# Attention and gated feed-forward on one core: final copy on two engines, a whole-tile store, GpSimd kept off two blocks, other buffers for two query parts, and new orders

## The chip, the core and the metric

The kernel runs on one core of a Trainium2 chip. The core has five engines that run side by side, each with its own queue of instructions taken strictly in order: TensorE (PE in the profile; PEld is its loading of weights), VectorE (DVE), ScalarE (ACT), GpSimd (POOL) and SyncE (SP). An instruction that waits for a semaphore holds up everything behind it on its engine. Matmuls write to PSUM, and the other engines read it from there; all else lies in SBUF. Transfers to and from memory run on 16 DMA engines and are issued by SP, ACT and POOL. The metric is the time of one execution in microseconds (us), taken over several runs.

## What is computed

The reference has an attention part with a squared ReLU instead of a softmax, and a gated feed-forward part on its output:

```python
# q, k, v: 8 batches x 12 heads x 448 positions x 64, float32
scores = (1 / sqrt(64)) * q @ k.T
attn   = maximum(scores, 0) ** 2 / 448
a      = attn @ v                        # 8 x 12 x 448 x 64
x      = a as 3584 tokens x 768
g      = x @ w_gate                      # 768 x 1536
u      = gelu(g) * (x @ w_val)           # 3584 x 1536
out    = u @ w_out                       # 3584 x 768, float32
```

## The kernel before

**Tiling.** All matmuls work in bfloat16 on quarters of the array: a 64x64 block of weights in one row half and one column half, with 448 moving columns (384 for the output product). `mm` (line 409) issues one. A step issues a pair of them, one for each column half, in the same row half; the plan calls pairs of the upper row half `PE0` and of the lower one `PE1`, and TensorE is fully used while a pair of each runs at the same time. Both are in one queue.

**Stages.** For each batch, heads come in pairs and parts of four heads. `load_qk` (line 461) brings a part of queries and keys to a `qk16` tile (a ring of two buffers in `hpool`), `add_transposes` turns it (on TensorE for the batches 0 and 1 and one part of batch 2, line 676, else by a DMA from a regrouped copy `qkr` in `lpool`, line 518). `add_scores` makes 21 units of scores a batch; ScalarE's ReLU (line 743) and VectorE's square (line 752) turn each into `attnT`. `add_values` multiplies by `v` (one accumulator for each pair of heads) and a copy (lines 814, 825) leaves `xT`. `add_gate_value` makes the dense gate and value products of a block of 128 columns of the hidden layer; other blocks go, for two batches at a time, through `add_pair`, a seven-product scheme (Strassen's) with sums of weights (line 890) and of tokens (line 909). GELU is on ScalarE (lines 985, 1061); the multiply of gate by value (lines 990, 1066) leaves `uT`. In `add_pair` that multiply may also go to GpSimd for the last pair of batches (`b >= SPARED`, line 1006). `add_product` makes the output in 14 groups of two 128-token tiles, again with seven products each, named "1" to "7"; their sums are on VectorE (line 1177), the results are copied or added into `osb` (lines 1265, 1267) and stored (line 1286).

**What sets the order.** The whole program is laid out by `run_plan` when it is built: it places every step by assumed costs and landing times (`margin` is added to a load's assumed landing). Batch 0's front is placed by hand with times (`at` below 0 is before the first dense product); everything after it comes in the order of the string `LINE` (a priority list: "s" scores, "o" values, digits dense products, letters the seven-product units). The loads of weights ("w", "o" for the output weights), "q" and "v" parts come in the order of `LOADS`, all issued by GpSimd, in order. While TensorE would idle in the first 30 us, `fill` (line 583) puts in matmuls on a zero tile `held` (line 597).

**The end.** Unit "3" of the last group is the last to run. Its result is copied by ScalarE alone, and the last group's first tile is stored in column halves, the second tile in two stores of 64 rows, one issued by SP and one by ACT:

```python
        if final and name == "3":
            rd.other = None
        (DVE if added else ACT).append(rd)
        ...
            if final and t == t0:
                SP.append(Op("SP", 0.6, lambda: emit_store(0, nc.sync, cols), reads, prio=-1))
                ACT.append(Op("ACT", 0.5, lambda: emit_store(1, nc.scalar, cols), reads, prio=-1))
```

Of the kernel before, what the change touches and what calls it, by code (L numbers as in the profile page):

```python
# [12 lines left out]
a3 1 s 1 s s o s 2D4 0 s 1 o 0 2A1 s 0F5 o o 0 s f1 2 0F6 s s 0E3 2A3 2 0F4 0 o o o 0 0 0F3 o o o  # L13
0F7 s s 2 a4 1 c6 s s 0 s 0F1 s b1 o 5 d1 d4 6C6 2D6 s s s s 0E2 0F2 0 s c1 s s s s 0 0E5 a7 1 1 s
6F5 2C4 0E1 1 2B1 s 0E7 s 2 0 o 0 0 0E6 1 o 0 1 s 1 f7 s s 0 0E4 4B6 s a1 5 o c4 2 s s s 2F2 b2 s 0
a5 a2 s s s o 0 3 b3 2B4 1 1 s s s 4C4 4 0 s 1 2B5 3 s 1 s o s 1 s 2E7 s 0 c3 s k7 s b4 1 a6 2B2 1
1 6D4 o 1 2A5 2 c7 2D1 o 6A1 2D5 2F1 2 2C3 b7 b5 1 s d6 s s s 3 s 2F3 2B3 b6 2C1 s 4D1 c2 2 s s s
2A4 s 2E4 4A3 s e1 3 s 2E6 2C2 6D7 c5 2B6 2A2 4F6 f5 2 s 2F6 2D2 s 2B7 s 2A6 s s 2D3 o s 4D7 2 s
2C6 2D7 2C5 s 2A7 g2 o 3 s 2E1 4C1 2C7 s s 4F1 o d5 4C2 s s 2F4 d7 s s o 4C3 s s 2E2 h1 s 3 o 3 4E5
g1 3 g6 s e6 o 4A2 4A1 4A5 s s e5 g5 6D1 e2 s 2E3 2F7 s 2F5 2E5 4 4A4 s s 2 3 4D6 i7 s s 6B7 o s 4  # L20
2 4D4 6B1 d2 o o s f2 s e7 3 s s d3 e4 5 s 3 4D3 s s h6 s s o 5 e3 s 3 f3 6J5 s 6I1 4B3 o h5 4 4 f6
s s m6 s 6F6 g7 s g4 s s 4E1 6G1 4B1 6A3 s o h3 s f4 s 4 4 4B7 m4 s s 4A7 k1 4 s g3 s 4E6 4E3 4B2 s
n3 4A6 j3 o o 4C5 4 s 6K7 o 4C6 6G7 o j5 s 6A6 4D2 j6 i3 6E4 4B4 i1 s s s 4E2 4B5 s 4D5 s 4F3 6E5 o
h4 k5 4F7 j1 s 4 s 4F2 4C7 4 6D5 l7 6H5 4 6A2 s 6D3 o 5 s o s s 4F5 o 4E4 s 4F4 6I7 6F7 s s s o 4E7
6D6 s 6F1 h2 5 6H3 s 5 s s 5 s h7 m2 k3 6J1 5 s s s s 5 6B6 5 s o i6 6B2 6H6 6G2 6E7 o j2 5 i2 s s
s 6J2 6E1 k6 6B5 s s s i5 j7 i4 s 6K4 l6 6L1 j4 s s 6A7 m3 6B4 k4 o 6A5 6C4 6C7 6F4 6L3 6D2 6B3 6L7
n1 6E2 6C3 6K1 6C1 6A4 6C2 n6 m1 6E6 l3 n4 6K3 6I5 6J7 6L5 l4 6G3 6C5 6E3 6I3 m7 l1 6L2 6H1 6K6 6K2
l5 6H2 6I2 m5 6J3 6G6 n5 6F2 6L4 6F3 l2 6J4 6G4 6H4 6I6 6G5 n7 6H7 k2 6L6 6J6 6K5 6I4 n2
"""

LOADS = """
w q q w q v q w v w w v w q v q o v q o q v o o q v v q v v v q q v q v q v q q q v v q q v v q q v
v v
"""


class Op:

# [279 lines left out]
def kernel(  # L318
# [463 lines left out]
    def add_values(at, b, pr):  # L782
# [48 lines left out]
        if last:  # L831
# [7 lines left out]
            for hi in ops[1]:  # L839
                pairs.append(("with", ops[0][1], hi))  # L840
# [717 lines left out]
```

## Time and profile before

| | us |
|---|---|
| median of three runs (lowest, highest) | 399.46 (398.38, 400.58) |
| the profiled execution, its own time | 399.09 |
| its span, from first to last instruction | 397.3 |
| TensorE busy in the first 60 us | 56.98 |
| TensorE busy from 60 to 380 us | 318.99 of 320 |
| TensorE busy from 380 us to the end | 12.52 of 17.3 |
| ScalarE, VectorE, GpSimd busy over the span | 254.9, 314.6, 98.5 |

The profile is of one execution. "Busy" is the time in which at least one instruction of an engine runs; since up to four quarter matmuls run together, TensorE can be busy and still do little, so the count of matmuls in a stretch (the number behind x) belongs to it. A releaser behind `<-` is what ended the idle time before an instruction. `L` numbers are lines of the kernel that the profile was taken of. In a timeline a row may stand for several instructions that followed each other.

### The profile page before, as it was taken

To read this page: it belongs to the slowest core of one execution; us is meant where nothing else is said; L and a number is where in the kernel's file an instruction comes from. 1 tells how busy PE (TensorE), PEld (TensorE's weight loads), DVE (VectorE), ACT (ScalarE), POOL (GpSimd) and SP (SyncE) were. 2 spreads that over 40 slices of the span, in tenths; PEclk is the share of its full clock that TensorE was granted. 3 is DMA by queue.
4 is the path that set the end of the run, shared out by engine and by line. 5 is a ranking of instruction groups with operands and counts; after the bars stand their busy time and mean duration, and the time that the engine had idled before them with its cause. 6 is when DMAs were issued, how large, how long until landed. Compare 5 with 4: busy or idle time off the path is not lost.

```text
span 397.3 us, 18514 instructions
## 1 busy us (share of the span) xinstructions
PE 388.5 (98%) x8411; PEld 334.7 (84%) x8414; DVE 314.6 (79%) x539; ACT 254.9 (64%) x387; POOL 98.5 (25%) x144
## 2 busy tenths in 40 slices
PE   7999999999999999999999999999999999999995
PEld 3555869999989988888999989999999977778894
DVE  2886898699876877989867879888989898759652
ACT  4957877576677666785766757777777464553220
POOL 8548441250320130120300403121000023254200
PEclk9999999999999999999999999999999999999998
DMA  7999999798796594564749988656622420000056
GB/s 98 171 198 179 197 199 146 102 173 140 95 219 97 113 198 70 89 93 51 108 101 191 139 203 129 99 84 98 74 40 73 111 54 3 3 2 3 22 124 179
DMA packets 75054, 44.38 MB, mean 112 GB/s; under 512 B 34400, under 2 KB 71520, under 8 KB 74976
## 3 DMA queue, kind: packets, MB, share of 16 engines
q0 software_dynamic: 38784, 24.39, 44.8%
q1 hardware_dynamic: 35632, 17.64, 22.1%
q8 instruction: 66, 1.08, 1.1%
q10 hardware_dynamic: 560, 1.18, 0.8%
q14 instruction: 12, 0.10, 0.1%
HBM read 48.76 MB, written 11.01 MB: 150 GB/s over the span
## 4 chain that ended last, share of the span: by engine, by line
PE 94%; ACT 2%; issue 1%; POOLq 1%; DMA 1%; POOL 1%; DVE 0%
PE ff L409 82%; PE sp L409 8%; ACT attnT L743 1%; PE sp L676 1%; PE ff L597 1%; PE ff L1465 1%; POOLq L1553 1%; DMA out_dram<-osb 1%; POOL uT L990 1%; PE ff L676 1%; PE ff L639 0%; DVE osb L1265 0%; ACT gel L985 0%; ACT qkT L647 0%; ACT osb L1267 0%
## 5 line engine op out<-in xcount | busy, mean ns | idle before, releaser
L743 ACT ACTIVATE attnT<-sp 128x896 bf16<-128x896 f32 x168 | 151.3, 922 | 45.0 <-PE sp L409 41.1
L409 PE MATMUL ff<-xT,wg 64*64 64x448 bf16 x1680 | 173.2, 349 | 0.0
L409 PE MATMUL ff<-xT,wv 64*64 64x448 bf16 x1056 | 114.1, 349 | 0.0
L409 PEld LDWEIGHTS <-wv 64*64 64x64 bf16 x1680 | 96.1, 107 | 9.9
L409 PEld LDWEIGHTS <-wg 64*64 64x64 bf16 x1680 | 95.1, 106 | 9.8
L752 DVE TENSOR_TENSOR attnT<-attnT 128x1792 bf16<-128x1792 bf16 (+1 forms) x98 | 92.2, 952 | 8.4 <-ACT attnT L743 7.7
L409 PE MATMUL ff<-attnT,v 64*64 64x448 bf16 (+1 forms) x768 | 83.2, 326 | 0.1
L409 PE MATMUL sp<-qkT 64*64 64x448 bf16 (+1 forms) x768 | 75.0, 328 | 1.3 <-ACT qkT L647 0.6
L409 PEld LDWEIGHTS <-s 64*64 64x64 bf16 x1200 | 71.5, 107 | 2.1 <-issue 0.2
L409 PE MATMUL ff<-ts,wv 64*64 64x448 bf16 x624 | 70.6, 349 | 0.0
L409 PEld LDWEIGHTS <-uT 64*64 64x64 bf16 x912 | 54.0, 107 | 3.2 <-POOL uT L990 1.1
L486 POOL DMA_DIRECT2D v<-in_v_dram x48 | 29.8, 634 | 105.7 <-ACT attnT L743 54.0
L981 DVE TENSOR_TENSOR part<-ff,part 128x448 f32<-128x448 f32 x78 | 47.2, 620 | 10.5 <-PE ff L409 7.5
L409 PE MATMUL ff<-ts,ws 64*64 64x448 bf16 x480 | 54.4, 349 | 0.0
L409 PE MATMUL ff<-wo,s 64*64 64x384 bf16 x576 | 53.9, 323 | 0.0
L409 PE MATMUL ff<-wt,s 64*64 64x384 bf16 x624 | 53.7, 322 | 0.0
L409 PEld LDWEIGHTS <-v 64*64 64x64 bf16 x768 | 45.9, 107 | 4.4 <-issue 0.9
L409 PE MATMUL ff<-wo,uT 64*64 64x384 bf16 x576 | 48.4, 323 | 1.0 <-POOL uT L990 0.7
L409 PEld LDWEIGHTS <-ws 64*64 64x64 bf16 x720 | 40.8, 106 | 5.7
L409 PEld LDWEIGHTS <-qkT 64*64 64x64 bf16 x768 | 36.4, 106 | 8.8 <-issue 4.2
L977 ACT COPY part<-ff 128x448 f32<-128x448 f32 x55 | 29.0, 532 | 21.7 <-PE ff L409 17.8
L471 POOL DMA_DIRECT2D qk<-in_q_dram x26 | 16.4, 631 | 97.3 <-ACT attnT L743 32.5
(76 smaller groups left out, 506.2 us busy)
## 6 DMA issues: line engine op xcount, KB each, us to landing
out_dram<-osb SPq DMA_DIRECT2D x49, 192.0 KB, 3.7
v<-in_v_dram POOLq DMA_DIRECT2D x48, 128.0 KB, 5.3
qk<-in_q_dram POOLq DMA_DIRECT2D x22, 224.0 KB, 5.3
qk<-in_k_dram POOLq DMA_DIRECT2D x22, 224.0 KB, 6.1
wg<-in_moe_w_gate_dram POOLq DMA_DIRECT2D x6, 384.0 KB, 10.0
wv<-in_moe_w_val_dram POOLq DMA_DIRECT2D x6, 384.0 KB, 11.0
wo<-in_moe_w_out_dram POOLq DMA_DIRECT2D x8, 288.0 KB, 8.8
out_dram<-osb ACTq DMA_DIRECT2D x5, 192.0 KB, 3.3
```

The costliest lines, as they stand in the source:

```text
L409: return nc.tensor.matmul(o, lhsT, rhs, start=start, stop=stop, skip_group_check=onto, tile_position=(P * row, P * col))
L471: op = load(4 * (h1 - h0) * S * D, lambda: nc.gpsimd.dma_start(tile_of(), src[b, h0:h1].rearrange("h (p c) d -> p h (c d)", c=SC)), deps, ...
L486: return nc.gpsimd.dma_start(v16[b, m][HALF[i], :, :, :], v[b, h0:h1].rearrange("h (p c) d -> p h c d", c=SC)[:, :, c0:c0 + VC, :])
L597: nc.tensor.matmul(t[:, :], warm[:, 0:128], warm[:, :], start=True, stop=True)
L676: nc.tensor.transpose(t[HALF[j], c, :], src[:, 2 * r + j, c, :], ident[:, :], tile_position=(0, P * j))
L743: relu.ins = nc.scalar.activation(duo["a"][:, u % 2, :, :], box[0][:, :, 0:S], AF.Relu).ins
L752: nc.vector.tensor_tensor(a[:, part], a[:, part], a[:, part], op=ALU.mult)
L977: rd.ins = copy(st["t", name][:, :], box[0][:, 0:S]).ins
L981: rd.ins = nc.vector.tensor_tensor(t[:, :], box[0][:, 0:S], t[:, :], op=ALU.add).ins
L990: return engine.tensor_tensor(uT[to][:, fc, :], st["g", g][:, :], st["t", of][:, :], op=ALU.mult).ins
L1465: nc.tensor.matmul(t[HALF[j], :], warm[:, HALF[j]], warm[:, :], start=True, stop=True, tile_position=(0, P * j))
L1553: with _tile.TileContext(nc) as tc:
```

## The change

Parts that can be told apart:

- The final copy (unit "3" of the last group) is cut in two halves of 192 columns, one for ScalarE and one for VectorE.
- The second tile of the last group is stored by one DMA of 128 rows issued by SP, instead of two of 64 rows.
- GpSimd may take the multiply of a seven-product unit only for blocks below `FC - 2`, so not for the last two blocks.
- The query-and-key parts (0, 2) and (1, 0) (batch, part) lie in buffers of `lpool` instead of `hpool`, and the ring of `hpool` counts without them.
- In batch 0's front, values of the head pairs 4 and 5 and the first products of gate and value get times of their own for each step (`SPOTS`, `FIRSTS`), the pairs 4 and 5 both in the split form that only pair 5 had; batch 1's first transposes come 0.6 later in the plan's time (`TURNS`).
- Two loads lose their margin in the plan.
- `LINE` and `LOADS` are new. In `LOADS` the v part of batch 1 comes one place earlier, the next one is ahead of the third pair of weights, and the last pair of weights goes from place 13 to place 17.
- `AHEAD1`, `TURN` and `SOON` are 0 or not used: they change nothing.

```diff
 LOADS = """
-w q q w q v q w v w w v w q v q o v q o q v o o q v v q v v v q q v q v q v q q q v v q q v v q q v
+w q q w v q q v w w w v o v q q w v q o q o o v q v v q v v q q v q q v q q v v q v q v v q q v v q
 v v
 """
...
+    STAGED = (0, 2), (1, 0)
+    AHEAD1, TURN = 0, 0
+    SPOTS = {(0, 4): (-16.7, -16.7, -14.2, -13.8), (0, 5): (-13.9, -13.9, -7.0, -6.9)}
+    FIRSTS = (-14.1, -14.1, -14.1, -14.05, -6.6, -6.2), (-7.3, -7.3, -7.3, -7.2, -6.5, -6.1)
+    TURNS = 0.65
+    SOON = -6.4, -6.3, -6.2
...
-                qk16[b, m] = hpool.tile([128, 4, SC * D], bf16, name="qk16", tag="qk16")
+                pool, tag = (lpool, "qkr") if (b, m) in STAGED else (hpool, "qk16")
+                qk16[b, m] = pool.tile([128, 4, SC * D], bf16, name="qk16", tag=tag)
...
-        order = ([0, 3, 1, 2] if pr % 2 else [0, 1, 2, 3], [3, 0, 1, 2])
-        last = (b, pr) == (0, NPAIR - 1)
+        last = (b, pr) if (b, pr) in SPOTS else None
+        order = ([0, 3, 1, 2] if pr % 2 else [0, 1, 2, 3], [0, 1, 2, 3] if last and not pr % 2 else [3, 0, 1, 2])
+        final, turn = ((0, order[0][3]), 2 + (pr % 2 == 0)) if last else ((1, VC - 2), 4)
...
-            ops[0][2].deps.append(ops[1][3])
-            for i in range(2):
-                lower.append((at - 0.6, ops[0][i]))
-                lower.append((at, ops[0][i + 2]))
+            ops[0][turn].deps.append(ops[1][3])
+            for i, x in enumerate(SPOTS[last]):
+                lower.append((x, ops[0][i]))
...
-                   other=("GPS", 1.05, lambda: emit(nc.gpsimd)) if b >= SPARED else None)
+                   other=("GPS", 1.05, lambda: emit(nc.gpsimd)) if b >= SPARED and fc < FC - 2 else None)
...
-            at = [PLACE5 - 0.5 + 0.1 * g] * 3 + [0.01 * g] * 3
+            at = [*FIRSTS[g]]
...
         if final and name == "3":
-            rd.other = None
+            half = OGS // 2
+            rd.cost, rd.other = 0.28, None
+            rd.emit = lambda: nc.scalar.copy(osb_of(t)[:, OGS:OGS + half], box[0][:, 0:half])
+            reads.append(Op("DVE", 0.31, lambda: nc.vector.tensor_copy(osb_of(t)[:, OGS + half:], box[0][:, half:OGS]),
+                            rd.deps, lag=0.2, prio=0))
+            DVE.append(reads[1])
...
+            elif final and len(st["done", t]) == 2:
+                def emit_both():
+                    (b, c), _ = chunks[1]
+                    rows = out[b * S:(b + 1) * S, :].rearrange("(p c) d -> c p d", c=SC)
+                    nc.sync.dma_start(rows[c:c + 2, :, :], osb[t][:, :])
+                SP.append(Op("SP", 0.6, emit_both, st["done", t], lag=2.5, prio=-1))
+                SP[-1].stored = 1.2
...
-        op.margin = LATE if kind == "w" and at < 5 or kind in "qv" and at <= (2, 0) else LATER_BY
+        op.margin = 0.0 if (kind, at) in (("w", 0), ("q", (1, 0))) else LATE if kind == "w" and at < 5 or kind in "qv" and at <= (2, 0) else LATER_BY
...
-    work.append((PLACE5 + 0.05, 1, add_transposes, (1, 0, (0, 1))))
+    work.append((PLACE5 + TURNS, 1, add_transposes, (1, 0, (0, 1))))
...
-        for new, old in zip(thirds[ring:], thirds):
+        turns = [x for x in thirds if made is not qk_loads or x not in STAGED]
+        for new, old in zip(turns[ring:], turns):
```

55 lines of the change are left out of this document (30 added, 25 removed).

## Prediction

> **What bounds the kernel now.** I read the page first, for the share of each engine and the chain of work that ended last.
>
> ```profile
> span 397.3 us, 18514 instructions
> ...
> PE 388.5 (98%) x8411; PEld 334.7 (84%) x8414; DVE 314.6 (79%) x539; ACT 254.9 (64%) x387; POOL 98.5 (25%) x144
> ...
> PE 94%; ACT 2%; issue 1%; POOLq 1%; DMA 1%; POOL 1%; DVE 0%
> ```
>
> TensorE is busy 98% of the span and is 94% of the chain, so a gain can only come from time in which it stands idle or runs half filled. A matmul here uses a 64x64 quarter of the array; a pair covers the two column halves of one row half, and the array is full only while pairs of both row halves run side by side. "Busy" does not show that; the number of matmuls in a stretch does. So next the table of windows (us; busy us and count of each engine; granted clock, DMA share, GB/s):
>
> ```profile
> 0.00:40.00 40.00, 37.36 (x585) 20.22 (x592) 26.05 (x46) 26.57 (x34) 26.21 (x44) 1.00 1.17 162
> ...
> 20.00:30.00 10.00, 9.73 (x159) 5.77 (x156) 8.32 (x15) 5.28 (x7) 4.44 (x7) 1.00 1.35 197
> 30.00:40.00 10.00, 10.00 (x210) 6.00 (x208) 6.34 (x9) 7.19 (x10) 8.35 (x12) 1.00 1.29 181
> 40.00:50.00 10.00, 10.00 (x224) 8.67 (x216) 8.72 (x14) 8.58 (x13) 4.15 (x6) 1.00 1.45 197
> 50.00:60.00 10.00, 9.62 (x182) 6.91 (x181) 9.39 (x15) 7.46 (x11) 4.39 (x7) 1.00 1.40 199
> 60.00:70.00 10.00, 10.00 (x226) 9.60 (x220) 8.36 (x12) 7.97 (x12) 0.79 (x2) 1.00 0.94 147
> ...
> 360.00:370.00 10.00, 10.00 (x238) 9.17 (x234) 10.00 (x24) 3.71 (x8) 4.46 (x4) 1.00 0.01 3
> ```
>
> From 60 us on the array takes 226 matmuls of 448 columns in 10 us, 22.6 per us, which I use as the full rate (238 per 10 us late, where they have 384 columns). Before that, in the first 60 us, it is starved; after it, one hole near 371 us and the tail are left. Those are the three places that the change can reach.
>
> **GpSimd kept off the last two blocks.** Four multiplies of the last pair of batches (blocks 10 and 11) may no longer go to GpSimd. The timeline around the hole, the groups by line, and TensorE's waits:
>
> ```profile
> 361.81 1.04 POOL L990 TENSOR_TENSOR uT<-gel,part 128x448 bf16<-128x448 bf16 x1 [2.45 <-ACT gel L985]
> ...
> 368.04 0.54 ACT L985 ACTIVATE gel<-ff 128x448 bf16<-128x448 f32 x1
> ...
> 368.66 2.58 POOL L990 TENSOR_TENSOR uT<-gel,part 128x448 bf16<-128x448 bf16 x1 [3.29 <-ACT gel L985]
> ...
> 371.27 0.36 DVE L1177 TENSOR_TENSOR qk<-uT 128x128 bf16<-128x128 bf16 x2 [0.93 <-POOL uT L990]
> ...
> L990 DVE TENSOR_TENSOR uT<-gel,part 128x448 bf16<-128x448 bf16 x34 | 21.2, 635 | 1.0 <-ACT gel L985 0.5
> ...
> 370.00:372.00 2.00, 1.29 (x32) 0.76 (x27) 1.07 (x4) 0.42 (x1) 1.24 (x1) 1.00 0.00 0
> ```
>
> The last multiply took 2.58 us against 1.04 of one before it, and TensorE stood until 371.3: 2.00 - 1.29 = 0.71 us lost. On VectorE it takes 0.64 us and can start when its input is done, 368.04 + 0.54 = 368.6, so it is there by 369.3 if VectorE has room. VectorE is full (10.00 of 10.00) from 360 to 370, but it then idled 0.93 us for this very multiply, which is more than the 0.64 it now carries. So what it pushes back still ends earlier than now. I take -0.7; ends: 0.0 (the sums at L1177 that are pushed back are needed first, and 0.64 of 0.71 comes back) and -0.9 (VectorE's wait goes whole).
>
> **The tail: final copy on two engines, a whole tile in one store.** The timeline of the last 6 us, and the copies of two widths on each engine:
>
> ```profile
> 391.36 1.16 PE L409 MATMUL ff<-wo,qk 64*64 64x384 bf16 x12
> ...
> 391.04 2.13 ACTq L1286 DMA_DIRECT2D out_dram<-osb  x2
> ...
> 393.21 0.48 ACT L1267 COPY osb<-ff 128x384 f32<-128x384 f32 x1 [4.24 <-DMA out_dram<-osb]
> 393.72 0.50 ACTq L1286 DMA_DIRECT2D out_dram<-osb  x1
> ...
> L1267 ACT COPY osb<-ff 128x384 f32<-128x384 f32 x34 | 16.3, 479 | 27.2 <-PE ff L409 22.7 <-DMA out_dram<-osb 4.2
> ...
> L977 ACT COPY part<-ff 128x448 f32<-128x448 f32 x55 | 29.0, 532 | 21.7 <-PE ff L409 17.8 <-POOL uT L990 3.0 <-DVE uT L990 0.2
> ...
> L1267 DVE COPY osb<-ff 128x384 f32<-128x384 f32 x22 | 12.2, 556 | 9.7 <-PE ff L409 9.3
> ...
> L977 DVE COPY part<-ff 128x448 f32<-128x448 f32 x23 | 14.3, 623 | 6.5 <-PE ff L409 5.1 <-ACT gel L985 0.6 <-POOL uT L990 0.5
> ```
>
> The last matmul ends at 391.36 + 1.16 = 392.52, yet the final copy starts at 393.21: ScalarE was still issuing two stores ahead of it (391.04 + 2.13 = 393.17). That is 0.69 us on the end. In the new order the tile whose sums end late is stored whole by SyncE alone, and ScalarE's last issue ahead of the copy is of a tile copied 12 matmuls before the end; it should be over when the copy may start. Against that stands how the two halves stand in the order: ScalarE's half waits for VectorE's semaphore, with the value of VectorE's own half, so they run one behind the other. From the two widths, 64 columns cost 0.067 us on VectorE and 0.053 on ScalarE; a half of 192 is then 0.556 - 0.201 = 0.36 and 0.479 - 0.159 = 0.32, together 0.68 us where one copy took 0.48, and some 0.05 for the hand-over: +0.25. Sum -0.69 + 0.25 = -0.4. Ends: -0.7 (halves side by side, 0.36, and no delay) and +0.25 (ScalarE again a long issue ahead). The whole-tile store, 384 KB, goes out ahead of the last two and its landing is hidden behind them.
>
> The page "PSUM — Partial Sum Buffer" of the Trainium skill (PSUM bank collisions raise a hardware error) says that two engines may not read one bank over the same partitions at once, columns apart or not. By that rule the halves cannot run side by side and the best end above is out; no run here has shown such a pair yet. It is the third rival below.
>
> **The front: two query parts in other buffers, orders of the first 28 us.** GpSimd issues all loads in one queue; the rows where it stood for a buffer, and what stood behind:
>
> ```profile
> 20.20 0.61 POOL L471 DMA_DIRECT2D qk<-in_q_dram  x1 [3.75 <-PE ff L676]
> ...
> 28.44 0.64 POOL L471 DMA_DIRECT2D qk<-in_q_dram  x1 [5.36 <-PE sp L676]
> ...
> 32.41 0.86 POOL L449 DMA_DIRECT2D wg<-in_moe_w_gate_dram  x1
> ...
> wg<-in_moe_w_gate_dram POOLq DMA_DIRECT2D x6, 384.0 KB, 10.0
> ...
> 25.69 0.35 PE L409 MATMUL ff<-xT,wv 64*64 64x448 bf16 x2
> ...
> 25.88 0.35 PE L409 MATMUL ff<-xT,wv 64*64 64x448 bf16 x2
> ...
> 27.16 0.97 PE L676 MATMUL sp<-ident,qk 128*64 128x128 bf16 x28
> ...
> 24.00:28.00 4.00, 3.89 (x78) 2.49 (x70) 3.19 (x6) 1.28 (x2) 0.00 (x0) 1.00 1.36 199
> ```
>
> The new buffers take the first of these waits away and let the second start its turn later in the list. But the DMA moves 181 to 199 GB/s from 20 to 60 us whether GpSimd stands or not, so the loads behind gain only the dip of the 30 to 40 window, (197 - 181) / 197 x 10 = 0.8 us; I book it at nothing: rival 1 finds 1.4 us of delay for one load in the new list. What helps directly is that in the new order ten pairs of the first gate and value products stand ahead of batch 1's transposes (27.16) instead of six, in place of filler matmuls on `held`, which only keep the array busy. Pairs of one row half follow each other by 25.88 - 25.69 = 0.19 us, so four pairs are 0.76 us of work moved into a stretch that has room: the 78 matmuls of 24 to 28 us are 28 transposes (0.97 us) and 50 others (50 / 22.6 = 2.2 us), 0.8 us short of 4.00. Two of the four pairs stand right ahead of the transposes and wait for a copy; they push batch 1's scores back by up to 0.4. I take -0.5; ends -0.8 and +0.4.
>
> **The middle: scores, weights and the new order up to 60 us.**
>
> ```profile
> 49.68 5.77 ACT L743 ACTIVATE attnT<-sp 128x896 bf16<-128x896 f32 x7
> ...
> 50.00:52.00 2.00, 1.88 (x32) 0.99 (x28) 2.00 (x4) 2.00 (x3) 0.61 (x1) 1.00 1.44 195
> 52.00:54.00 2.00, 1.74 (x24) 1.22 (x26) 2.00 (x3) 2.00 (x4) 0.61 (x1) 1.00 1.45 197
> ```
>
> Seven score units of batch 1 come so close in TensorE's order (matmuls 755 to 853, 98 of them, 4.3 us at full rate) that ScalarE's seven activations, 5.77 us without a gap, set the pace. In 50 to 54 us only 56 matmuls ran where 90 fit: 34 / 22.6 = 1.5 us lost. In the new order the same units stand at 716 to 852: 136 matmuls, 6.0 us, just above 5.77. So ScalarE's pace no longer binds: -1.5. The price is in the order too: between matmuls 600 and 900 ten more pairs have no partner of the other row half, each 0.19 / 2, +0.9. Sum -0.6; ends -1.5 (the lone pairs fall where it would wait anyway) and +0.9 plus what the first rival adds. From 60 to 360 us both orders come from the same planner, and the one there now loses almost nothing (226 per 10 us); I book nothing there.
>
> **Sum.** -0.7 - 0.4 - 0.5 - 0.6 = -2.2. The profiled execution took 399.09 us (span 397.3 and 1.8 around it): 396.9. The median of the runs, 399.46, lies 0.37 above it, so 397.3 for the median of the changed kernel.
>
> **Rivals.**
> 1. Weights set the pace, and it gets slower. The third weight pair is issued at 32.41 and lands 10.0 later, 42.4. Its first reader is matmul 649 of the order; 585 had run by 40 us, so it comes at 40 + 64 / 22.6 = 42.8: 0.4 of slack. In the new load order a value part (two of 128 KB, at 181 to 197 GB/s 1.4 us) goes ahead of it, while its reader moves back only to matmul 670, 0.9 us: 0.1 short. If GpSimd's earlier turn does not make that up, what the front wins is waited away here (and its worse end, +0.4, may stand), every score queued behind waits too, the 1.5 of the middle is not won and the lone pairs stay: -0.7 - 0.4 + 0.9 + 0.1 + 0.4 = +0.3, 399.8. It decides once that pair lands over 1.3 us later than 42.4. Its far end is a like case at the output weights:
>
> ```profile
> 87.62 0.77 POOL L458 DMA_DIRECT2D wo<-in_moe_w_out_dram  x1 [1.11 <-DMA wo<-in_moe_w_out_dram]
> ...
> wo<-in_moe_w_out_dram POOLq DMA_DIRECT2D x8, 288.0 KB, 8.8
> ```
>
> The last part lands at 96.4; its first reader is matmul 1843 now and 1796 then, 2.1 us earlier. A load queue that comes 3 us later there would cost another 1.7: 401.5. For it: both weights sit close to their readers. Against it: waits of the queue are removed in front of them.
> 2. Middle and front come to nothing (the lone pairs eat it, the transposes move back), and only the hole at 371 and the tail are won: -1.1, 398.4. For it: ScalarE and DMA stay as full as now.
> 3. The two-engine copy does not do what it says: the halves in series, and ScalarE late as now: +0.25 in place of -0.4, 397.9.
>
> **How the numbers follow.** Forecast 0.55, with its own range 396.1 to 398.5; rival 1 0.16, rival 2 0.21, rival 3 0.08. The least difference that a measurement of this kernel can tell from no change is about 0.5%, 2.0 us (its three runs span 398.38 to 400.58), so faster means below 397.5. Of the forecast two thirds lie there (0.37), of rival 2 0.05, of rival 3 0.03: 0.45. Slower means above 401.5: the far half of rival 1 (0.08), and 0.04 of the forecast for an unseen wait in the 300 us of new order: 0.12. The rest, 0.43, is no change. The best ends together (-0.9 - 0.7 - 0.8 - 1.5 = -3.9) give 395.6; upwards I go past rival 1's 399.8: 395.5 to 400.2.
>
> **What would show it.** Right: no POOL multiply after 367 us and over 230 matmuls in the 10 us after 365; 24 to 28 us with over 82 matmuls; 50 to 54 us with over 75, and ScalarE's activations with gaps there; the final store issued about 0.8 us after the last matmul instead of 1.2. Wrong: TensorE waiting for a weight load near 43 or 97 us, a new wait on L1177's counterpart after 368 us, or a final ScalarE half that starts over 0.8 us after the last matmul. The forecast as a whole is wrong if the stretch from 20 to 60 us loses as much as before.

## The result, and the profile after

| | before | changed |
|---|---|---|
| median of the runs, us (lowest to highest, runs) | 399.55 (398.38 to 400.58, 6) | 406.27 (404.51 to 406.69, 6) |
| ratio to before | | 1.016, 95% interval 1.0134 to 1.0186 |
| profiled execution, us; its span | 399.09; 397.3 | 406.5; 404.6 |
| last matmul's end, from the timeline | 392.52 | 393.87 |
| from there to the end of the span | 4.80 | 10.77 |

The changed kernel is 1.6% slower; 397.3 was forecast, with a range up to 400.2. The last two rows say where to look. Of the 7.3 us by which the span grew, 6.0 lie behind the last matmul, where only the final copy and the stores are left, and 1.35 lie ahead of it.

The page of the changed kernel, with the chain of work that ended last:

```profile
span 404.6 us, 18488 instructions
...
PE 390.1 (96%) x8413; PEld 339.3 (84%) x8413; DVE 321.7 (80%) x552; ACT 250.9 (62%) x377; POOL 96.1 (24%) x142
...
PE 96%; DVE 1%; issue 1%; ACT 0%
```

TensorE's busy time hardly moved, but its share fell from 98% to 96%: the span has a piece in which it does nothing. The timeline of the changed kernel's last 14 us, engine by engine (start, length, what was done, idle time before it and its releaser):

```profile
391.63 2.24 PE L415 MATMUL ff<-wo,qk 64*64 64x384 bf16 x34
...
393.91 0.36 DVE L1289 COPY osb<-ff 128x192 f32<-128x192 f32 x1 [1.50 <-PE ff L415]
...
394.30 0.32 ACT L1288 COPY osb<-ff 128x192 f32<-128x192 f32 x1 [1.00 <-DVE osb L1289]
394.65 0.50 ACTq L1298 DMA_DIRECT2D out_dram<-osb  x1
...
391.47 0.62 SPq L1310 DMA_DIRECT2D out_dram<-osb  x1
393.33 2.67 SPq L1298 DMA_DIRECT2D out_dram<-osb  x2
```

All engines have issued their last by 396.0, and the kernel ends 8.6 us later. What is under way then are stores. The view of the DMA queues of the changed kernel, from 399 to 402 us and then from 391 to 403.2 us (for a queue: packets, MB, the time of its packets as a share of 16 engines; for an issue: count, size, median us to landing):

```profile
DMA packets 52, 0.15 MB, mean 50 GB/s; under 512 B 2, under 2 KB 5, under 8 KB 52
...
q1 hardware_dynamic: 47, 0.14, 12.1%
...
out_dram<-osb SPq DMA_DIRECT2D x1, 384.0 KB
...
out_dram<-osb SPq DMA_DIRECT2D x1, 96.0 KB, 8.8
out_dram<-osb ACTq DMA_DIRECT2D x1, 96.0 KB, 5.2
```

The same view of the kernel before, from 392 to 395.8 us:

```profile
DMA packets 480, 0.79 MB, mean 207 GB/s; under 512 B 96, under 2 KB 352, under 8 KB 480
...
q1 hardware_dynamic: 240, 0.39, 48.0%
q10 hardware_dynamic: 240, 0.39, 32.8%
...
out_dram<-osb SPq DMA_DIRECT2D x1, 96.0 KB, 2.2
out_dram<-osb ACTq DMA_DIRECT2D x1, 96.0 KB, 2.4
```

Before, the stores at the end keep the 16 engines some 80% busy (48.0% on SP's queue, `q1`, and 32.8% on ScalarE's, `q10`) at 207 GB/s. After, the rate is 50 GB/s and SP's queue uses 12.1% of 16 engines, which is two engines: 2 / 16 = 12.5%. The packets of 3072 bytes, one per row of the tile, run two at a time from 392.68 to 402.84, most of them 121 ns each. 128 rows make 64 x 0.121 = 7.7 us on two engines; it took 10.2 because a few packets at the start took up to 0.5 us, and other stores' packets seem to have come in between. Of the 64 packets of the last store of 96 KB on the same queue, 56 end by 398.65; the other 8 come only behind the whole tile's, from 402.66 to 403.09, and so this store takes 8.8 us to land instead of 2.2.

Ahead of the last matmul, the windows answer to those shown of the kernel before:

```profile
20.00:30.00 10.00, 9.80 (x160) 5.43 (x154) 8.28 (x15) 5.29 (x7) 3.39 (x6) 1.00 1.37 200
30.00:40.00 10.00, 10.00 (x208) 6.80 (x207) 6.11 (x9) 7.23 (x10) 8.62 (x12) 1.00 1.26 177
40.00:50.00 10.00, 10.00 (x204) 8.36 (x197) 9.11 (x15) 8.16 (x12) 2.78 (x4) 1.00 1.45 196
50.00:60.00 10.00, 10.00 (x202) 7.74 (x195) 9.27 (x15) 6.87 (x10) 3.50 (x6) 1.00 1.16 171
...
140.00:150.00 10.00, 9.14 (x203) 7.64 (x199) 7.44 (x12) 5.04 (x7) 3.25 (x6) 1.00 1.13 207
...
320.00:340.00 20.00, 19.44 (x407) 16.19 (x405) 17.16 (x29) 11.40 (x22) 7.33 (x7) 1.00 0.09 23
...
365.00:375.00 10.00, 10.00 (x245) 9.09 (x242) 8.14 (x25) 3.01 (x6) 1.91 (x2) 1.00 0.02 3
```

```profile
140.00:150.00 10.00, 10.00 (x226) 8.69 (x221) 8.10 (x13) 6.63 (x9) 3.05 (x5) 1.00 0.96 175
...
320.00:340.00 20.00, 20.00 (x429) 14.52 (x424) 17.17 (x30) 10.65 (x22) 6.38 (x6) 1.00 0.03 9
...
365.00:375.00 10.00, 9.29 (x228) 8.39 (x223) 7.54 (x24) 2.94 (x6) 2.95 (x2) 1.00 0.01 2
```

The second fence holds the rows of the kernel before that were not shown. Read the counts of matmuls. From 20 to 60 us the four rows add up to 774 against 775 before (a matmul that runs across a border counts in both rows): 20 fewer at 40 to 50, 20 more at 50 to 60. So the new front is another order of the same loss. At 365 to 375 the hole is gone: 17 more matmuls, 0.7 us at the 24.5 per us that run there. In exchange 22 are missing at 320 to 340 (1.0 us) and 23 at 140 to 150 (1.0 us). These two holes are new.

### The profile page after: what moved, and what is told of

Read it like the earlier page. It is cut to its first block, busy times and chain, and to the rows that moved or that the text cites. A ratio compares the mean times of both kernels' runs of the same rounds, so it can differ in the third digit from the quotient of the medians.

```text
span 404.6 us, 18488 instructions
## 1 busy us (share of the span) xinstructions
PE 390.1 (96%) x8413; PEld 339.3 (84%) x8413; DVE 321.7 (80%) x552; ACT 250.9 (62%) x377; POOL 96.1 (24%) x142
## 3 DMA queue, kind: packets, MB, share of 16 engines
q8 instruction: 66, 1.08, 1.1%
## 4 chain that ended last, share of the span: by engine, by line
PE 96%; DVE 1%; issue 1%; ACT 0%
PE ff L415 83%; PE sp L415 9%; PE ff L604 1%; PE sp L683 1%; PE ff L1488 1%; PE ff L683 1%; DVE uT L997 0%; DVE part L988 0%; PE ff L646 0%; DVE qkr L897 0%; DVE part L984 0%; ACT qkT L654 0%; DVE wv L897 0%; DVE osb L1289 0%; ACT osb L1288 0%
## 5 line engine op out<-in xcount | busy, mean ns | idle before, releaser
L415 PE MATMUL ff<-xT,wg 64*64 64x448 bf16 x1680 | 171.2, 349 | 0.2 <-issue 0.2
L415 PE MATMUL ff<-xT,wv 64*64 64x448 bf16 x1056 | 116.8, 349 | 0.9 <-issue 0.9
L415 PEld LDWEIGHTS <-wv 64*64 64x64 bf16 x1680 | 101.9, 106 | 10.2 <-issue 0.5
L415 PEld LDWEIGHTS <-wg 64*64 64x64 bf16 x1680 | 99.8, 106 | 11.0 <-issue 2.0
L415 PEld LDWEIGHTS <-uT 64*64 64x64 bf16 x912 | 55.9, 107 | 1.6
L415 PE MATMUL ff<-wt,s 64*64 64x384 bf16 x624 | 55.3, 322 | 0.0
L415 PE MATMUL ff<-wo,uT 64*64 64x384 bf16 x576 | 54.7, 322 | 0.0
L415 PEld LDWEIGHTS <-v 64*64 64x64 bf16 x768 | 47.8, 107 | 4.4 <-issue 1.2
L415 PEld LDWEIGHTS <-ws 64*64 64x64 bf16 x720 | 44.5, 106 | 5.4 <-issue 0.9
L1274 ACT COPY osb<-ff 128x384 f32<-128x384 f32 x33 | 15.7, 479 | 30.9 <-PE ff L415 24.5
## 6 DMA issues: line engine op xcount, KB each, us to landing
wv<-in_moe_w_val_dram POOLq DMA_DIRECT2D x6, 384.0 KB, 10.6
```

Source lines behind the costliest of these rows:

```text
L415: return nc.tensor.matmul(o, lhsT, rhs, start=start, stop=stop, skip_group_check=onto, tile_position=(P * row, P * col))
L1274: ins = copy(o, box[0][:, 0:OGS])
```

## Experiments

Every run stands beside runs of the kernel before on the same chip, and a ratio is to those; their median was 399.29 for the four runs of the first section below; 399.67 for the exclusion alone, the exclusion undone, no GpSimd multiply at all and the row stores on SP's queue; and 399.60 for the other four. Runs with different medians ran on different chips, so a difference of some 0.3% between their ratios is not clear of the noise. Where a hole or a tail is compared, it is read from the profiled execution.

### The tail: what holds the stores up

**Two row stores.** In the changed kernel, the whole-tile store is written as two stores of 64 rows each, on the same queue:

```diff
-                nc.sync.dma_start(rows[c:c + 2, :, :], osb[t][:, :])
-            SP.append(Op("SP", 0.6, emit_both, st["done", t], lag=2.5, prio=-1))
+            for j in range(2):
+                SP.append(Op("SP", 0.6, lambda j=j: emit_store(j, nc.sync), st["done", t], lag=2.5, prio=-1))
```

> The changed kernel, with its whole-tile store written as two stores of 64 rows each, both on SP's queue; all else is the changed kernel. Theory A (the whole-tile store is served by two DMA engines): in the trace of the changed kernel, from 398.4 us on, its packets of 3072 bytes run two at a time, 121 ns each, up to 402.72, and the last store's packets of 1536 bytes end behind them at 403.09; two row stores spread over more engines, the packets end near 397, and the span falls from 404.6 to 398.9 (398.2 to 399.8). Rival B (too many bytes on one queue at the end: SP's queue has 384 KB and 96 KB in the last 2 us): the bytes on SP's queue stay, and the span stays at 404 to 405. Rival C (the wait of ScalarE's half copy for VectorE's half): the tail stays, 404 to 405, since that copy still ends near 394.6.

400.00 us (398.95 to 404.16, 12 runs), ratio 1.0036, interval 1.0012 to 1.0060; span 397.2. The view of the DMA queues of this run, 392 to 395.6 us:

```profile
DMA packets 374, 0.72 MB, mean 199 GB/s; under 512 B 81, under 2 KB 209, under 8 KB 373
...
q1 hardware_dynamic: 213, 0.41, 47.3%
...
out_dram<-osb SPq DMA_DIRECT2D x1, 96.0 KB, 3.2
```

The queue is the same and so are the bytes, but SP's queue is back at 47.3% of 16 engines and the tail at 5.1 us. Theory A holds; rivals B (bytes on one queue) and C (the half copy's wait, which is still there) fall. The span lies below the 398.2 to 399.8 that theory A gave: this execution, the fastest of the twelve, has the hole at 332 us but neither of those near 96 and 147.

**Two column stores.** Also two issues, but each of all 128 rows and half of the columns (`part` is the left, then the right 384):

```diff
-                nc.sync.dma_start(rows[c:c + 2, :, :], osb[t][:, :])
+                nc.sync.dma_start(rows[c:c + 2, :, part], osb[t][:, part])
```

> The changed kernel, with its whole-tile store written as two stores on SP's queue, each of all 128 rows and half of the columns (packets of 1536 bytes, 65 ns each in the trace of the changed kernel). Theory A (two engines, because the destination's outermost dimension is 2): each store still has that dimension, 64 packets for each of the two engines and store, 2 x 64 x 65 ns = 8.3 us against 64 x 121 ns = 7.7 us for the whole one; span 404 to 406. Rival D (it is the size of one issue, 384 KB, that goes to few engines): issues of 192 KB spread, as those of 192 KB before did, and the span falls to about 399.

406.29 us (404.78 to 407.38, 4 runs), ratio 1.0167, interval 1.0141 to 1.0192; tail 10.6. The DMA queues of this run, 400 to 403 us:

```profile
q1 hardware_dynamic: 97, 0.15, 12.9%
```

Issues of 192 KB are as slow as one of 384 KB when the destination begins with a dimension of 2; the row stores have the same size and are not. So the shape decides and not the size: rival D falls. The two runs also differ in the rows of one issue (64 and 128), which no run takes apart from the destination's shape; that just two engines work is what points to its dimension of 2.

**The old tail.** In the changed kernel both edits of the tail are undone:

```diff
-            half = OGS // 2
...
-            DVE.append(reads[1])
+            rd.other = None
...
-            elif final and len(st["done", t]) == 2:
...
```

> The changed kernel with the tail of the kernel before: one whole final copy on ScalarE, and the last whole tile stored by two stores on two queues. What is left of the change is the orders, the buffers and GpSimd kept off the last two blocks. Theory A: without the whole-tile store the span is about that of the last matmul (393.9 in the changed kernel against 392.5) plus 4.8 as before, 398.7 (398.0 to 399.6), and it is 1 to 1.5 above the 397.3 of before, because TensorE stands 1.2 us at 146.5 and 0.5 us at 95.9 (each time the next weight load comes 1.3 to 1.6 us after a 16 KB packet of the instruction queue that is late has ended) and 0.6 to 0.8 us at 332 (VectorE's copy of a part ends 332.67). Rival E (those stalls are chance and not the orders'): they don't recur at the same matmuls, and the span is 396.5 to 397.5. The prediction's own sum without its tail term gave 397.3 - 1.8 = 395.5. B and C give no more than the tail's part: 398.9 too.

400.88 us (399.97 to 404.85, 11 runs), ratio 1.0041, interval 1.0016 to 1.0066; span 399.5, last matmul at 394.20, tail 5.3. Without the tail's edits the orders are not faster than the kernel before, and not at 395.5, as the prediction's sum has them. Rival E is half right: the hole at 332 came again, the one at 96 too, the one at 147 did not, and one at 205 was new.

**The whole-tile store alone**, put into the kernel before:

```diff
+            elif final and len(st["done", t]) == 2:
+                def emit_both():
...
+                    nc.sync.dma_start(rows[c:c + 2, :, :], osb[t][:, :])
```

> The kernel before, with the whole-tile store of the change alone (one store of 128 rows on SP's queue). Theory A: 128 packets on two engines, 64 x 121 ns = 7.7 us from about 394 on, with the last store's packets behind them: span 397.3 + 5 = 402.5 (401 to 404). Rival B: the bytes on SP's queue at the end grow from 288 to 480 KB, which at the 200 GB/s that all queues moved from 390 to 394 us is 1 us: 398.3. Rival C: no change, 397.3, or 0.4 less, as ScalarE is free for the last copy 0.69 us earlier.

406.11 us (405.00 to 406.40, 4 runs), ratio 1.0169, interval 1.0148 to 1.0191: this one edit is as slow as the whole change. The tail is 11.4 against 4.8, some 1.6 more than the theory's 5 extra, and the span of 404.5 lies past the 401 to 404 given: the store's packets ran from 393.75 to 402.66, 8.9 us and not 7.7. From 399 to 402 us:

```profile
q1 hardware_dynamic: 51, 0.16, 12.9%
```

### GpSimd off the last two blocks

**The exclusion alone**, in the kernel before:

```diff
-  other=("GPS", 1.05, lambda: emit(nc.gpsimd)) if b >= SPARED else None)
+  other=("GPS", 1.05, lambda: emit(nc.gpsimd)) if b >= SPARED and fc < FC - 2 else None)
```

> The kernel before, with GpSimd kept off the last two blocks of a batch and nothing else. Theory F (step A of the prediction): TensorE's hole at 370 to 372 us, of 0.7 to 1.0 in every execution of the kernel before and of its variant with the whole-tile store, goes, and nothing takes its place; the span of an execution without other stalls falls from 396.5 to 395.6 and the median from 399.3 to 398.4 (ratio 0.9978, 0.996 to 0.999). Rival G: the multiplies that GpSimd gives up come to VectorE at a time when it is 10.00 of 10 us busy, and another hole of the same size opens between 360 and 375; ratio 0.999 to 1.002.

398.87 us (398.35 to 400.65, 12 runs), ratio 0.9968, interval 0.9947 to 0.9990. Its interval lies below 1: it beats both kernels. Its windows:

```profile
365.00:375.00 10.00, 10.00 (x250) 9.01 (x244) 8.38 (x25) 3.58 (x8) 0.00 (x0) 1.00 0.05 11
```

250 matmuls where the kernel before had 228; the 22 are 0.9 us at the 25.0 per us that run there. Theory F holds, and no other hole of over 0.5 us opened.

**The exclusion undone in the new orders** (the edit above in reverse, in the changed kernel with two row stores):

> The changed kernel with two row stores on SP's queue, and GpSimd allowed again in all blocks. It differs from the run with two row stores alone from about 365 us on. Theory I: TensorE's hole at 330 to 333 us (0.75 to 0.95 in all four profiles of the new orders, where VectorE's uT multiply takes 1.46 instead of 0.61 beside three GpSimd multiplies in a row) belongs to the new orders and not to the exclusion, and stays; whether a hole comes back near 371 is what the exclusion is worth in these orders: up to 1.0, median 400.0 to 401.0. Rival J: the exclusion moved those three multiplies together; then the hole at 332 goes here, and the median is 399.0 to 400.0.

400.67 us (399.17 to 404.61, 12 runs), ratio 1.0011, interval 0.9983 to 1.0040. Its windows:

```profile
325.00:335.00 10.00, 9.45 (x195) 7.36 (x190) 9.62 (x15) 5.18 (x10) 4.42 (x4) 1.00 0.01 3
...
365.00:375.00 10.00, 10.00 (x245) 9.07 (x239) 7.64 (x22) 3.22 (x7) 3.55 (x4) 1.00 0.01 3
```

The hole at 332 stays, so it is the orders' own (theory I, against J). And no hole comes back at 371, although GpSimd multiplies there again (3.55 us): in the new orders the exclusion has nothing to win. What was predicted for two edits could be won only once.

### The hole at 332

The changed kernel's timeline around it, VectorE first, then GpSimd, and TensorE's matmul behind the hole:

```profile
327.40 1.08 DVE L897 TENSOR_TENSOR attnT<-wv 128x768 bf16<-128x768 bf16 x1
...
328.94 0.86 DVE L897 TENSOR_TENSOR attnT<-attnT,wg 128x768 bf16<-128x768 bf16 x1
329.73 1.46 DVE L997 TENSOR_TENSOR uT<-gel,part 128x448 bf16<-128x448 bf16 x1
331.11 0.55 DVE L897 TENSOR_TENSOR qkr<-wg,attnT 128x768 bf16<-128x768 bf16 x1
331.58 0.55 DVE L897 TENSOR_TENSOR wv<-wg,wv 128x768 bf16<-128x768 bf16 x1
332.05 0.61 DVE L984 COPY part<-ff 128x448 f32<-128x448 f32 x1
...
327.03 3.67 POOL L997 TENSOR_TENSOR uT<-gel,part 128x448 bf16<-128x448 bf16 x3 [1.56 <-DVE part L988]
...
332.71 0.56 PE L415 MATMUL ff<-ts,ws 64*64 64x448 bf16 x6 [0.56 <-DVE part L984]
```

VectorE's multiply takes 1.46 us instead of 0.61 while the third of GpSimd's multiplies runs (to 330.70), then two sums of weights go, and only then the copy of a part that TensorE waits for. The two sums shown ahead of it, also beside GpSimd's multiplies (327.03 to 330.70), take 1.08 and 0.86 us where the two behind it take 0.55. Over the whole trace of the changed kernel, the 37 such multiplies and 25 sums on VectorE that no GpSimd multiply overlaps take at most 0.63 and 0.56 us; the three multiplies that one overlaps by 0.9 us or more take 1.38 to 1.46, and each ends 0.48 us behind it.

**One multiply moved.** Feature block 1 of batch 7, the third of GpSimd's three, goes to VectorE; TensorE's order is the same:

```diff
-  other=("GPS", 1.05, lambda: emit(nc.gpsimd)) if b >= SPARED and fc < FC - 2 else None)
+  other=("GPS", 1.05, lambda: emit(nc.gpsimd)) if b >= SPARED and fc < FC - 2 and (to, fc) != (7, 1) else None)
```

> The changed kernel with two row stores on SP's queue, and one uT multiply (feature block 1 of batch 7, the third of the three that GpSimd takes in a row at 325 us) given to VectorE; TensorE's order is the same, and on VectorE its copy of a part moves ahead of one sum of weights. Theory I (VectorE's multiply takes 1.46 because GpSimd multiplies beside it, and what is behind it on VectorE, a copy of a part, comes too late for TensorE): VectorE's two multiplies there take 1.2 together, the copy ends 0.5 to 0.7 us earlier, and TensorE's hole at 330 to 333 falls from 0.95 to 0.2 to 0.45; median 0.5 to 0.75 below the 400.0 of the kernel that it is made from. Rival K (VectorE has simply too much to do there): the multiply added costs VectorE 0.6 more, the hole stays at 0.9 or grows, and the median stays at 400.0 or more.

399.68 us (398.78 to 401.77, 12 runs), ratio 1.0003, interval 0.9984 to 1.0023, where the kernel that it is made from had 1.0036. Its timeline of VectorE:

```profile
329.87 1.15 DVE L997 TENSOR_TENSOR uT<-gel,part 128x448 bf16<-128x448 bf16 x2
330.94 0.55 DVE L897 TENSOR_TENSOR qkr<-wg,attnT 128x768 bf16<-128x768 bf16 x1
331.41 0.61 DVE L984 COPY part<-ff 128x448 f32<-128x448 f32 x1
```

Two multiplies on VectorE are quicker (1.15) than one beside GpSimd (1.46), and the copy starts 1.54 us after the multiply's start instead of 2.32: 0.31 of that is the multiply, and 0.47 is one sum less ahead of the copy. From 320 to 340 us TensorE runs 423 matmuls instead of 406 in the kernel that this one is made from, and its list of waits has no entry there any more. Rival K falls. The median is 0.3 below that kernel's 400.0 where 0.5 to 0.75 was expected, and the two intervals overlap: the hole is shown to go, its price in the median is not. Nor do the runs say whether the quicker multiply alone, without the copy's new place ahead of a sum, would have closed it.

The page "SBUF — State Buffer" of the Trainium skill (SBUF: two separate sides) says that VectorE, with two inputs in that memory, and GpSimd take a shared port in turn, each for a whole instruction, and the other stands. By that rule the late 0.85 us is a wait for GpSimd's multiply; the trace agrees, in that the long VectorE multiply ends 0.5 us after GpSimd's third, about the length of one alone (0.61), and shrinks when that third is taken away.

**No GpSimd multiply at all**, also in the changed kernel with two row stores:

```diff
-  other=("GPS", 1.05, lambda: emit(nc.gpsimd)) if b >= SPARED and fc < FC - 2 else None)
+  other=("GPS", 1.05, lambda: emit(nc.gpsimd)) if b > 7 else None)
```

> The changed kernel with two row stores on SP's queue, and GpSimd making no uT multiply at all: all go to VectorE. Theory I (the hole at 332 is VectorE and GpSimd multiplying at once, 0.85 on one VectorE multiply): the slow multiplies of 1.46, 1.92 and 1.42 us are all 0.6 here and the hole at 332 goes; against it VectorE takes 16 more multiplies of 0.61 = 9.8 us in the 55 us after 320, where it has been idle some 6 to 8 us: the median is 399.5 to 402. Rival K (the hole comes from the order of VectorE's other work, its copy of a part at 332): the hole stays, and with the 9.8 us the median is 402 to 405.

409.05 us (408.44 to 410.26, 4 runs), ratio 1.0219, interval 1.0178 to 1.0259. VectorE's multiplies there take 0.6 each and the hole at 332 is gone (427 matmuls from 320 to 340 us), as theory I has it. (The 1.92 of the expectation is a row of two multiplies.) But the time misses both. VectorE is then busy 9.68 of 10 us from 365 to 375, where only 207 matmuls run; and the plan orders the last products otherwise, so that 76 run from 390 to 395 us and 36 from 395 to 400, where 132 and 126 did in the two stretches of 5 us before. The two were not told apart, so this run says little about what GpSimd is worth.

### The final copy and ScalarE's stores

**Row stores on SP's queue** in the kernel before, with the exclusion; the final copy is whole, on ScalarE:

```diff
+            elif final and len(st["done", t]) == 2:
+                for j in range(2):
+                    SP.append(Op("SP", 0.6, lambda j=j: emit_store(j, nc.sync), st["done", t], lag=2.5, prio=-1))
```

> The kernel before, with GpSimd kept off the last two blocks, and with the last whole tile's two row stores both on SP's queue, so that ScalarE issues neither before its final copy (which stays whole on ScalarE). Theory F, and the tail's part of the prediction without the whole-tile store: the hole at 371 gone (0.9), and the final copy starts at the last matmul instead of 0.69 behind it, so that the tail from the last matmul to the end falls from 4.8 to 4.3: median 399.3 - 0.9 - 0.5 = 397.9 (ratio 0.9965). Rival H: SP's two issues of 0.6 each hold up its final store by as much as ScalarE's copy gains, and the tail stays at 4.8: 398.4 (0.9978), the same as with GpSimd kept off alone.

399.02 us (397.81 to 400.08, 12 runs), ratio 0.9970, interval 0.9948 to 0.9993: not to be told from the exclusion alone. Its timeline of ScalarE, with the last matmul at 392.01:

```profile
392.05 0.48 ACT L1267 COPY osb<-ff 128x384 f32<-128x384 f32 x1 [5.48 <-PE ff L409]
392.56 0.49 ACTq L1286 DMA_DIRECT2D out_dram<-osb  x1
```

and SP's last issue in this run and, in the second row, in the kernel before:

```profile
393.23 0.74 SPq L1286 DMA_DIRECT2D out_dram<-osb  x1
...
393.72 0.47 SPq L1286 DMA_DIRECT2D out_dram<-osb  x1
```

The copy now starts 0.04 after the last matmul instead of 0.69, as the prediction wanted, and ScalarE's half of the last store is issued 0.55 after it instead of 1.20. Yet the tail is 5.17, against 5.11 with the exclusion alone and 4.80 before. SP issues the two row stores until 393.14, so its half of the last store goes out at 393.23, 1.22 after the last matmul as against 1.20 before; that is rival H, in its mechanism too. And its packets end 2.4 us after the issue instead of 1.8, so that the tail even grows.

**The copy on two engines** added to that:

```diff
-            rd.other = None
+            half = OGS // 2
+            rd.cost, rd.other = 0.28, None
...
+            DVE.append(reads[1])
```

> The kernel before with GpSimd kept off the last two blocks, the two row stores on SP's queue, and the final copy on two engines (VectorE's half, then ScalarE's); it differs from the run with GpSimd kept off and two row stores only in that copy. Theory: ScalarE's half ends some 0.7 to 0.8 after the last matmul in place of 0.5, and what ends the span is the stores' packets behind it, so that the tail from the last matmul to the end is 5.1 to 5.4 against 5.17, and the median 398.9 to 399.5 against 399.0. Rival (the two halves run side by side, as the change means): copy done 0.4 after the last matmul, tail 4.8 to 5.0.

399.39 us (398.50 to 400.53, 10 runs), ratio 0.9994, interval 0.9978 to 1.0010; tail 5.29. Its timeline, ScalarE and then VectorE, with the last matmul at 393.06:

```profile
393.09 0.32 ACT L1281 COPY osb<-ff 128x192 f32<-128x192 f32 x1 [5.47 <-PE ff L409]
393.83 0.47 ACTq L1291 DMA_DIRECT2D out_dram<-osb  x1
...
393.44 0.36 DVE L1282 COPY osb<-ff 128x192 f32<-128x192 f32 x1 [0.77 <-ACT osb L1281]
```

Here ScalarE's half goes first and VectorE's waits for it, the other way round than in the changed kernel, but again one behind the other. The copy is done 0.74 us after the last matmul, in place of 0.52 with one engine: +0.2, as expected. SP's half of the last store again waits for SP's own row stores and goes out at 394.30, 1.24 after the last matmul.

### The front

**Six pairs ahead**, in the changed kernel with two row stores:

```diff
-    FIRSTS = (-14.1, -14.1, -14.1, -14.05, -6.6, -6.2), (-7.3, -7.3, -7.3, -7.2, -6.5, -6.1)
-    TURNS = 0.65
+    FIRSTS = (-7.5, -7.5, -7.5, 0.0, 0.0, 0.0), (-7.4, -7.4, -7.4, 0.01, 0.01, 0.01)
+    TURNS = 0.05
```

> The changed kernel with two row stores on SP's queue, and the first gate and value pairs placed as in the kernel before: six ahead of batch 1's transposes instead of ten. Step C of the prediction: the four pairs taken ahead are worth 0.5; without them TensorE's lost time up to 60 us grows by 0.5 and the median from 400.0 to 400.5. Theory M (what is taken ahead at 20 to 25 us is missing at 25 to 30 and 40 to 50, since the kernels before and after have lost the same by 30 us, 17.3 and 17.2): the lost time up to 30 us stays within 0.2, and that up to 60 us and the median within 0.5 of 400.0, in either direction.

424.05 us (422.85 to 426.01, 4 runs), ratio 1.0614, interval 1.0580 to 1.0648. In 0 to 30 us it runs 357 matmuls where the kernel that it is made from runs 384: 27 / 22.6 = 1.2 us, more than either side expected, and theory M falls in this form. The rest comes later: 170 matmuls instead of 223 from 60 to 70 us, 1017 instead of 1116 from 150 to 200, 175 instead of 232 from 310 to 320. Why so much is lost there is not shown; the order by hand was made for other places of these pairs. So taking the four pairs back costs more in the new order than the prediction's 0.5, and yet new and old order run the same number of matmuls by 60 us (975 and 977): the old order filled that stretch with other work.

### The holes without a cause

TensorE's holes near 96, 118 and 147 us are put down to "issue" by the profile. Their places in TensorE's instruction stream, counted from the traces of all these runs from 60 us on, are alike: twenty of them, of 0.5 to 1.8 us from the start of one weight load to the next, all begin 0.73 to 0.74 of the way into a block of 256 instructions (17.73 blocks in at 118 us, 22.74 at 147 us), and each ends 1.24 to 1.58 us after a late 16 KB packet of the instruction queue has landed. Over all profiles, TensorE passes this place in a block 812 times. In 44 cases the packet had landed less than 1.6 us ahead, never less than 1.23, and all twenty holes are among them; in the other 768 no weight load at this place came more than 0.24 us after the one before. Fourteen are in seven profiles of the new orders, five in the six of the old, and one in the run with six pairs ahead. The page "Runtime: NRT & Kernel Launch" of the Trainium skill (Instruction fetch mechanics) says that instructions are refilled in blocks of 16 KB, 256 instructions, and that this is mostly hidden. The trace agrees on the 256 and on the "mostly": at twenty places of the 812 it is not hidden.

**A load twice.** In the kernel before with the exclusion, the query and key part (4, 0) is loaded once more, to a place that nothing reads:

```diff
+        def emit():
+            if (b, m) == (4, 0):
...
+                nc.gpsimd.dma_start(twice["t"][HALF[i], :, :], src[b, h0:h1].rearrange("h (p c) d -> p h (c d)", c=SC))
```

> The kernel before with GpSimd kept off the last two blocks, and the query and key part that is loaded at 109.6 to 110.9 us loaded twice (once more to a place in memory that nothing reads). TensorE's order is the same. Theory L (TensorE's holes without a named cause are loads of its own instructions, 16 KB each, that stand behind data on the DMA engines): 0.46 MB more are written at the 150 to 200 GB/s seen there, 2.3 to 3 us; the instruction packet that ended at 116.7 to 117.5 in the kernel before and its variants ends 1.5 to 3 us later, and the hole at 118, 0.3 to 0.9 in four profiles, grows to 1.5 to 4, at the same matmul; median 398.9 + 1.5 to 3 = 400.4 to 401.9. Rival N (those holes have nothing to do with data on the DMA engines): the hole stays at 0.3 to 0.9 and the median at 398.5 to 399.3.

399.76 us (398.40 to 401.26, 10 runs), ratio 0.9998, interval 0.9981 to 1.0014, against 0.9968 without it. The hole at 118 did not grow (0.63 between weight loads; 0.79, 1.12 and 0.79 in three other profiles of the old order, and under 0.5 in two). A second one came at the next block, at 124.4, which no other profile of the old orders has at that place:

```profile
125.06 0.38 PE L409 MATMUL sp<-qkT 64*64 64x224 bf16 x5 [0.18 <-issue]
```

The packet for it landed at 123.69 instead of 121.10 in the kernel that this one is made from, while the doubled loads kept the DMA engines full to about 122.5 instead of 120. So theory L missed in place and size, N in place and time. That data in front makes instruction packets late fits all of this, but with one profile it isn't settled, and this profile has a hole of 0.61 us at 46.6 as well, at the same place in a block and long before the doubled loads. That the holes are late instruction packets is read from where they stand and when the packets land; no run changed the packets alone.

## Why the prediction was wrong

**The step that failed** is the last sentence on the tail: "The whole-tile store, 384 KB, goes out ahead of the last two and its landing is hidden behind them." Its bytes were counted and its shape was not. On two engines its packets take 10.2 us, and the last packets of the last store wait behind them. As the term of the sum, the tail was booked at -0.4 with a worst end of +0.25; it is +6.0 in the profiles, and +6.7 by the ratio of the kernel before with that edit alone (0.0169 x 399.3). A step for what the destination of each store looks like, 2 x 64 x 768 with the 2 outermost, would have asked the question. The page "DMA: Bandwidth & Descriptors" of the Trainium skill (Why a DMA increments its semaphore by 16 and not by 1) has the answer: the number of engines is the largest up to 16 that divides the outermost size above 1 on both sides, here 2. The trace agrees (12.1 and 12.9% of 16).

**GpSimd off the last two blocks.** Right in the old orders: -0.7 taken, 0.9 found in the windows, ratio 0.9968. The mechanism stands, a late multiply on GpSimd with room on VectorE. What was missed is that the new orders lose that hole by themselves. The sign given, no GpSimd multiply after 367, did not come (one runs at 374.01, but TensorE waits for none there); over 230 matmuls in 365 to 375 did (245).

**The tail apart from the store.** The freed ScalarE (-0.69) came as described when tried alone, and the halves in series (+0.25) cost 0.2. The sign given came too: in the changed kernel the final store is issued at 394.65, 0.78 after the last matmul instead of 1.20. But the end is set by when the last store's packets are through, and that did not come earlier: the tails are 4.8 to 5.3 in all versions without the whole-tile store. With both row stores on SP, its queue holds up the last store in the old order (1.22); in the changed kernel with two row stores the last store goes out 0.77 after the last matmul, and its packets take 2.7 us instead of 2.0. Why they take longer is open; 384 KB of other stores are issued 0.5 us before the last matmul there, and 192 KB in the kernel before. So the -0.4 was a gain that the stores took back: rival 3's result, for another reason than rival 3's. The page "PSUM — Partial Sum Buffer" of the Trainium skill (PSUM bank collisions raise a hardware error) has the rule of one bank and two engines that the prediction weighed: the halves ran one behind the other in every profile, the second released by the first one's semaphore, so no run here shows two engines at one bank.

**Front and middle.** -0.5 and -0.6 were taken; together they are 0 (975 matmuls against 977 by 60 us). Their rows in the changed kernel:

```profile
24.00:28.00 4.00, 3.80 (x64) 2.14 (x59) 3.23 (x6) 1.29 (x2) 1.22 (x2) 1.00 1.39 198
50.00:54.00 4.00, 4.00 (x76) 3.28 (x67) 4.00 (x8) 4.00 (x6) 1.23 (x2) 1.00 1.36 200
...
27.65 0.97 PE L683 MATMUL sp<-ident,qk 128*64 128x128 bf16 x28
```

The middle's sign came only in part: 76 matmuls in 50 to 54 us against 56, as wanted, but ScalarE is busy all of the 4 us as before and 20 matmuls are missing at 40 to 50. In the front 24 to 28 us hold 64 matmuls, not over 82. The pairs did come in (20 gate and value matmuls instead of 12), but the transposes start at 27.65 instead of 27.16, so that 16 of their 28 fall behind 28 us, and six matmuls of values went elsewhere; from 20 to 30 us the counts are 160 and 159. Both steps priced what moves in and not what moves back or out. This was rival 2's case for these stages. The waits for weights near 43 and 97 us of rival 1 didn't come: the third weight pair lands at 42.80 instead of 42.20, less than the 1.3 us later at which rival 1 decides, TensorE's list of waits has none, and the hole at 96 is at a block of instructions.

**"From 60 to 360 us I book nothing there."** This was the second error. Ahead of the last matmul the new order lost 1.0 at 332 us and in this execution some 1.0 at 147 and 0.3 at 96, against 0.7 won at 371. The first comes in all five profiles of the new orders that leave GpSimd's three multiplies there as they are; the others come and go between kernels that are alike up to there. That they make up the 0.4% by which the changed kernel with its store mended is above the kernel before is likely but not shown: without the hole at 332 the ratio was 1.0003, in an interval that overlaps with that kernel's.

## What to carry to other kernels

Read the outermost dimension of both sides of a transfer before you merge two into one: 64 rows and 64 rows were spread over the engines, one store of 2 x 64 rows ran on two of them, and at the end of a kernel nothing hides it. Price what a reordered stretch gives up as well as what it takes in, by counting matmuls over the whole stage. And where two edits aim at one hole, try each alone: here no version did better than the one-line exclusion by itself (0.9968), and the rest of the change cost more than it brought.

## What the hardware showed that was not expected

- A store of 384 KB with an outermost dimension of 2 moved at 50 GB/s (two of 16 engines), and a store of 96 KB behind it on the same queue took 8.8 us to land in place of 2.2, for the last 8 of its 64 packets.
- A VectorE multiply of two inputs took 1.46 us instead of 0.61 beside GpSimd's, and sums took up to 1.10 instead of 0.55; two multiplies on VectorE alone took 1.15.
- By all signs here TensorE stood for its own instructions: holes of 0.5 to 1.8 us at one place in a block of 256, all where a 16 KB instruction packet had landed less than 1.6 us before, in some profiles and not in others of kernels that are alike up to there. Single profiles of versions that differ by 1 us can't be ranked without counting them.
